# A memory-augmented recurrence beside a dense layer: ring of five places and 20 streamed units in place of six and 21, with parts of the attention later and the last eviction on two engines

## The chip, the cores and the metric

The kernel runs on one core of one Trainium2 chip. The metric is the device time of one execution in microseconds; the median of three runs before the change is 2274.5 us (2267.7 to 2279.35). A core has a matrix engine (TensorE, "PE"; "PEld" is its loading of weights), VectorE ("DVE"), ScalarE ("ACT"), GpSimd ("POOL") and SyncE ("SP"), which here only issues transfers. Matrix products accumulate in PSUM[...]; all other tiles lie in SBUF.

## The reference

The output is the sum of the input x, a recurrent attention over segments of 32 rows, and a dense layer with a gelu. The recurrent part decides the shape of the kernel. x has 2048 rows of 1024, so there are 64 segments; each has 8 rows of memory ahead of its 32 rows, and the memory rows of its output are the memory of the next segment.

```python
xn = _layernorm(x)
mem = mem0                                   # (1, 8, 1024)
for s in range(64):
    h = concatenate([mem, xn[:, 32*s:32*s+32]], axis=1)       # 40 rows
    q, k, v = (einsum('btd,dhe->bhte', h, W) for W in (Wq, Wk, Wv))   # 32 heads of 128
    scores = where(mask, einsum('bhqe,bhke->bhqk', q, k) * 128 ** -0.5, -1e9)
    o = einsum('bhqk,bhke->bhqe', softmax(scores), v)
    o = einsum('bhte,hed->btd', o, Wo)
    mem = o[:, :8]                           # the next segment waits for this
    outs.append(o[:, 8:])
return x + concatenate(outs, axis=1) + (gelu(xn @ w1 + b1) @ w2 + b2)
```

Wq, Wk, Wv and Wo are 8 MB each in bf16. They are needed whole in each of the 64 segments, and not all of the 32 MB fits into SBUF beside the rest.

## The kernel before

The dense layer comes first, up to about 443 us. Then the recurrence runs, segment after segment. A segment passes through 64 weight units of 512 KB in a fixed order: the first halves of K, Q and V (8 units each), the second halves of K, Q and V, then 16 units of the output product. Most units are resident in SBUF. The others, marked S in a string of 64 places, are streamed from DRAM each time through a ring of places. The ring and the residents share the same space: 41 places of one size and 8 late ones, 49 in all, so each place taken from the ring holds one more resident unit.

```python
STREAMED = 21
STREAM_BUFS = 6
PLACED = "S..S...S" "...S..S." "..S..S.." "S...S..S" "..S..S.S" "..S..S.." "S..S..S." ".S..S..S"
# the fourth streamed unit of a pass is kept in PSUM and put into its place from there
IN_PSUM = [unit for unit in ORDER if IS_STREAMED[unit]][3]

    def start_stream():
        if started < len(streams):
            t = slab(STREAM_PLACES[started % STREAM_BUFS])
            if streams[started] == IN_PSUM and "kept" in nxt:
                nc.scalar.copy(out=t[:, 0:1024], in_=nxt["kept"][:, 0, :])            # line 190
                nc.vector.tensor_copy(out=t[:, 1024:2048], in_=nxt["kept"][:, 1, :])  # line 191
            else:
                nc.sync.dma_start(out=t[:, :], in_=copies[streams[started]])          # line 193
            stream_tiles.append(t)
            started += 1

    def unit_done(unit):
        if IS_STREAMED[unit]:
            start_stream()       # the place just used takes the next unit that isn't under way
            ...
```

A half pass multiplies 24 rows of the segment and the 8 memory rows with eight units. The rows that a segment leaves over (8 of its 32) are gathered for four segments and go through one of the passes again with their own accumulator: with K when the segment's number is 0 modulo 4, in the output product at 1, with Q at 2 and with V at 3. The small work of the attention is put between units by number:

```python
    for i in range(KT):                       # 8 units
        t = unit_tile((w, i, u))
        product(i, t, hT, ps, range(KT))      # 4 matmuls, line 598
        if left and i not in ahead:
            product(i, t, hL, psL, order)
        unit_done((w, i, u))
        for fn in at.get(i, ()):              # small work after unit i
            fn()
```

The small work: `turn_*` turns evicted rows by four transposes into PSUM (line 555) and VectorE copies them out (lines 642 to 652); `scores` builds the scores and ScalarE takes the exponential (line 696); `sums` adds them up by a product, then a logarithm and an exponential on ScalarE (708, 709) and two products on VectorE (710, 711); `values` multiplies by V (722, 728) and both engines evict (734, 735); `keep_q` copies queries of the left rows aside (667).

```python
            at = {1: [sums]}                                # in the second half of K
            if left_q and not first:
                at[3] = [lambda: keep_q(0)]
                at[5] = [lambda: turn_qL(st["natL"], 0)]
            psK1, psK1L = half_pass("K", 1, left_k, at)
            ...
            at = {1: [sums], 4: [lambda: values(1, 0)], 6: [lambda: values(1, 1)]}   # in the output product
            ...
            for n, unit in enumerate(O_UNITS):              # 16 units
                t = unit_tile(unit)
                o_product(unit, t, psX)                     # 8 or 4 matmuls, line 746
                unit_done(unit)
                for fn in at.get(n, ()):
                    fn()
                if n == 7 and not st.get("res"):
                    load_res("e", nc.scalar)
            nw = 2 if left_o else 1                         # left_o: with left rows, one segment in four
            if not final:
                o_sb = HOME["d"]
                nc.scalar.copy(out=o_sb[:, 0:256], in_=psX[:, 0:256])                  # line 840
                if left_o:
                    nc.vector.tensor_copy(out=o_sb[:, 256:512], in_=psX[:, 256:512])   # line 842
                put_mem(o_sb, nxt["hT"], tr, 4 // nw)       # transposes (222), VectorE's copy (223)
```

`put_mem` writes the new memory rows into the rows of the next segment (`hr`), so the next segment's first product waits for it.

Of the kernel before, what the change touches and what calls it, by code (L numbers as in the profile page):

```python
# [17 lines left out]
S = 2048  # L18
# [23 lines left out]


NUNIT = 64
STREAMED = 21
STREAM_BUFS = 6


def pass_order():

    order = []

    for u in range(2):
        for w in ("K", "Q", "V"):
            for i in range(KT):
                order.append((w, i, u))
    for ch in range(2):
        for j in range(4):
            for u in range(2):
                order.append(("O", ch * 4 + j, u))  # L60
    return order


ORDER = pass_order()
PLACED = "S..S...S" "...S..S." "..S..S.." "S...S..S" "..S..S.S" "..S..S.." "S..S..S." ".S..S..S"
IS_STREAMED = {unit: PLACED[n] == "S" for n, unit in enumerate(ORDER)}
assert PLACED.count("S") == STREAMED
RESIDENT = [unit for unit in ORDER if not IS_STREAMED[unit]]

IN_PSUM = [unit for unit in ORDER if IS_STREAMED[unit]][3]  # L70
assert len(RESIDENT) == NUNIT - STREAMED


@with_exitstack
def kernel(
# [16 lines left out]
    nc = tc.nc  # L92
# [28 lines left out]
    def slab(place):  # L121
        return slabs.tile([P, 2048], BF16, name="u", tag=place)
# [14 lines left out]
    for m, n, base in ((mask_order[0:NX, 0:NX], NX, 0), (mask_order[0:SEG, NX:SEG], NL, NX)):  # L137
        nc.gpsimd.affine_select(
            out=m, in_=m, pattern=[[1, n]], compare_op=ALU.is_ge, fill=MASKED, base=base, channel_multiplier=-1,
# [3 lines left out]
        out=m, in_=m, pattern=[[-8, GRP]], compare_op=ALU.is_ge, fill=MASKED, base=0, channel_multiplier=1,  # L143
    )
    nc.gpsimd.affine_select(
        out=m, in_=m, pattern=[[8, GRP]], compare_op=ALU.is_ge, fill=MASKED, base=7, channel_multiplier=-1,
# [10 lines left out]
    PLACES += [f"w2_{k}" for k in range(14)] + [f"gT{k}" for k in range(7)]  # L157
    STREAM_PLACES, RES_PLACES = PLACES[:STREAM_BUFS], PLACES[STREAM_BUFS:]
    res_tiles = {}
# [25 lines left out]
    def start_stream():  # L185
        nonlocal started
# [3 lines that stand above are left out]
                nc.scalar.copy(out=t[:, 0:1024], in_=nxt["kept"][:, 0, :])  # L190
                nc.vector.tensor_copy(out=t[:, 1024:2048], in_=nxt["kept"][:, 1, :])
            else:
                nc.sync.dma_start(out=t[:, :], in_=copies[streams[started]])
            stream_tiles.append(t)
            started += 1
# [34 lines left out]
    with tc.tile_pool(name="ma", bufs=2) as ma, tc.tile_pool(name="mps", bufs=6, space=PSUM) as mps:  # L230
# [11 lines left out]
        o_sb = HOME["d"]  # L242
# [131 lines left out]
        for tg in range(4):  # L374
# [13 lines left out]
            for fb in range(FC):  # L388
                ps = mps.tile([P, 512], F32, name="ps")
                for kt in range(KT):  # L390
# [9 lines left out]
                    out=xb[:, :], in_=ps[:, :], func=ACT.Identity, bias=b1col[:, fb:fb + 1], scale=1.0  # L400
# [4 lines left out]
                    out=u[:, :], in0=u[:, :], scalar1=0.044715, scalar2=1.0, op0=ALU.mult, op1=ALU.add  # L405
# [47 lines left out]
            else:  # L453


                for _ in range(STREAM_BUFS):
                    start_stream()
# [35 lines left out]
    with tc.tile_pool(name="late", bufs=1) as late, \  # L493
# [16 lines left out]
        def let_go(ps):  # L510
            free_banks.append(bank_of.pop(id(ps))[0])
# [40 lines left out]
        def turn4(nat, dst):  # L552

            for c in range(4):
                nc.tensor.transpose(dst[:, c, :], nat[:, c * P:(c + 1) * P], ident[:, :])  # L555

        def by_head(t):
            return t.rearrange("p c (j t) -> p (c j) t", j=4)
# [8 lines left out]
        for s in range(NSEG):  # L567
# [14 lines left out]
            left_o = i4 == 1 or final  # L582
# [3 lines left out]
            st = {}  # L586
# [34 lines left out]
            def home(tag, pool=sp):  # L621
                return HOME[tag][:, 0:512] if tag in HOME else pool.tile([P, 512], BF16, name="natL", tag=tag)[:, :]
# [7 lines left out]
            def left_out(psL, tag, pool=sp):  # L630
                nat = home(tag, pool)
                nc.vector.tensor_copy(out=nat[:, :], in_=psL[:, :])  # L632
                let_go(psL)
                return nat

            def left_values(u, ps):
                VL[u] = left_out(ps, f"VL{u}", late)
# [6 lines left out]
            def turn_kL(nat, u):  # L644
                turn4(nat, tr)
                kL[u] = sp.tile([P, 16, 32], BF16, name=f"kL{u}")
                nc.vector.tensor_copy(out=kL[u][:, :, :], in_=by_head(tr))
# [6 lines left out]
            def turn_qL(nat, u):  # L654
                turn4(nat, qL[:, 4 * u:4 * u + 4, :])
# [9 lines left out]
            def keep_q(u):  # L665

                nc.vector.tensor_copy(
                    out=qS[:, u, :, :], in_=by_head(qL[:, 4 * u:4 * u + 4, :])[:, :, 3 * NL:4 * NL]
                )
# [44 lines left out]
            def values(u, r):  # L714

                V, prA, prB = st["V"], st["prA"], st["prB"]
                av = [new_acc() for _ in range(2)]
                oV = [t[:, 0:160].rearrange("p (c q) -> p c q", q=40) for t in av]
                for c in range(4):
                    for b in range(2):  # L720
                        q = slice(64 * r + 32 * b, 64 * r + 32 * b + 32)
                        nc.tensor.matmul(  # L722
                            oV[b][:, c, :], lhsT=V[q, c * P:(c + 1) * P], rhs=prA[q, c, :],
                            start=(c == 0), stop=False, skip_group_check=True, tile_position=(64 * r + 32 * b, 0),
                        )
                    for b in range(2):
                        q = slice(64 * r + 32 * b, 64 * r + 32 * b + 32)
                        nc.tensor.matmul(  # L728
                            oV[b][:, c, NX:40], lhsT=VL[u][q, c * P:(c + 1) * P], rhs=prB[q, c, :],
                            start=False, stop=True, skip_group_check=True, tile_position=(64 * r + 32 * b, 0),  # L730
                        )
                for b, cp in enumerate((nc.scalar.copy, nc.vector.tensor_copy)):
                    hs, t0 = slice(8 * r + 4 * b, 8 * r + 4 * b + 4), SEG + NL * slot
                    cp(out=(o_both if left_o else o_main)[u][:, hs, 0:32], in_=oV[b][:, :, 0:32])  # L734
                    cp(out=o_both[u][:, hs, t0:t0 + NL], in_=oV[b][:, :, 32:40])
                    let_go(av[b])
# [21 lines left out]
            at = {3: [lambda: turn_k(nat)]}  # L758
# [5 lines left out]
            at = {2: [lambda: turn_q(natq)], 6: [lambda: scores(0)]}  # L764
# [9 lines left out]
                left_values(0, psVL)  # L774


            at = {1: [sums]}
            if left_q and not first:
                qS = sp.tile([P, 2, 16, NL], BF16, name="qS")
                at[3] = [lambda: keep_q(0)]  # L780
                at[5] = [lambda: turn_qL(st["natL"], 0)]
            psK1, psK1L = half_pass("K", 1, left_k, at)
            natk1 = rows_out(psK1, "d")
            at = {2: [lambda: turn_k(natk1)], 4: [lambda: values(0, 0)], 6: [lambda: values(0, 1)]}
            if left_k:
                at[2].append(lambda: st.update(natL=left_out(psK1L, "d")))
                at[4].insert(0, lambda: turn_kL(st["natL"], 1))
            if left_v and not first:
                at[6].append(lambda: left_values(0, psVL))
            psQ1, psQ1L = half_pass("Q", 1, left_q, at)  # L790
            natq1 = rows_out(psQ1, "b")
            at = {3: [lambda: turn_q(natq1)], 6: [lambda: scores(1)]}
# [20 lines left out]
            psV1, psV1L = half_pass("V", 1, left_v, at)  # L813
# [4 lines left out]
                load_x_rows(s + 1, nc.gpsimd)  # L818


            at = {1: [sums], 4: [lambda: values(1, 0)], 6: [lambda: values(1, 1)]}
            if left_v and not first:
                at[6].append(lambda: left_values(1, psV1L))
            if left_q and not first:
                at[7] = [lambda: keep_q(1)]
                at[8] = [lambda: st.update(natL=left_out(psQ1L, "d"))]
                at[11] = [lambda: turn_qL(st["natL"], 1)]
            psX = new_acc()
            for n, unit in enumerate(O_UNITS):
                t = unit_tile(unit)  # L830
                o_product(unit, t, psX)
                unit_done(unit)
                for fn in at.get(n, ()):
                    fn()
                if n == 7 and not st.get("res"):
                    load_res("e", nc.scalar)
            nw = 2 if left_o else 1
            if not final:
                o_sb = HOME["d"]
                nc.scalar.copy(out=o_sb[:, 0:256], in_=psX[:, 0:256])  # L840
                if left_o:
                    nc.vector.tensor_copy(out=o_sb[:, 256:512], in_=psX[:, 256:512])
                put_mem(o_sb, nxt["hT"], tr, 4 // nw)
            res, rows = st["res"], slice(s * SEG, s * SEG + NX)
            tiles = (res, st["resL"]) if left_o else (res,)
# [12 lines left out]
            if final:  # L858
                engines = [nc.sync, nc.scalar, nc.gpsimd]
                n = 0  # L860
# [62 lines left out]
```

The softmax here doesn't subtract the row's maximum and nothing guards it: scores larger than these inputs give would overflow.

## Time and profile before

| what | before |
|---|---|
| time, median of 3 runs | 2274.5 us |
| span of the profiled execution | 2273.2 us |
| TensorE busy, share of the span | 2028.4 us, 89% |
| weight loads busy | 1047.3 us, 46% |
| VectorE busy | 828.8 us, 36% |
| ScalarE busy | 660.5 us, 29% |
| GpSimd busy | 269.6 us, 12% |
| moved by DMA | 761.91 MB |
| products of the half passes (line 598, rows of the segment) | 12288 matmuls, 939.8 us |

The page is of one execution. A busy share is an average over the dense part and the recurrence, which have different limits, so the prediction reads the recurrence by itself. Matmuls overlap: four of 32 columns each run side by side, and the busy time of TensorE is that of their union, with modelled ends. In a line of a view, "L598" is line 598 of the kernel, "acc<-u,hr" says that the tile acc is written from u and hr, and "<-" after a wait names what ended it. Numbers of columns in a shape are elements per partition. "issue" is time in which an engine waited for nothing that the profile shows. "SPq" is SyncE's queue, which issues the stream.

### The profile page before, as it was taken

To read this page: it belongs to the slowest core of one execution; us is meant where nothing else is said; L and a number is where in the kernel's file an instruction comes from. 1 tells how busy PE (TensorE), PEld (TensorE's weight loads), DVE (VectorE), ACT (ScalarE), POOL (GpSimd) and SP (SyncE) were. 2 spreads that over 40 slices of the span, in tenths; PEclk is the share of its full clock that TensorE was granted. 3 is DMA by queue.
4 is the path that set the end of the run, shared out by engine and by line. 5 is a ranking of instruction groups with operands and counts; after the bars stand their busy time and mean duration, and the time that the engine had idled before them with its cause. 6 is when DMAs were issued, how large, how long until landed. Compare 5 with 4: busy or idle time off the path is not lost.

```text
span 2273.2 us, 79002 instructions
## 1 busy us (share of the span) xinstructions
PE 2028.4 (89%) x34707; PEld 1047.3 (46%) x34707; DVE 828.8 (36%) x2264; ACT 660.5 (29%) x1540; POOL 269.6 (12%) x527
## 2 busy tenths in 40 slices
PE   7999999888898988898989898989898889888986
PEld 3444444344444444444544444444444444444443
DVE  6574844133333333333333333333323333333332
ACT  5251623122222222222222222222222222222222
POOL 0000000024111011111111111010111111111110
PEclk9999999999999999999999999999999999999999
DMA  9621116899999999999999999999999999999997
GB/s 323 205 71 33 51 51 230 296 395 391 388 402 371 384 373 388 362 382 386 386 379 401 377 397 374 395 372 374 376 372 372 376 383 400 378 379 378 401 382 276
DMA packets 256629, 761.91 MB, mean 335 GB/s; under 512 B 50923, under 2 KB 68283, under 8 KB 256284
## 3 DMA queue, kind: packets, MB, share of 16 engines
q1 hardware_dynamic: 234748, 736.71, 85.3%
q0 software_dynamic: 16000, 16.87, 2.2%
q8 instruction: 271, 4.44, 0.8%
q10 hardware_dynamic: 5536, 3.30, 0.5%
q14 instruction: 74, 0.61, 0.1%
HBM read 742.52 MB, written 33.10 MB: 341 GB/s over the span
## 4 chain that ended last, share of the span: by engine, by line
PE 66%; DMA 24%; DVE 3%; issue 3%; ACT 3%; POOL 0%; ACTq 0%; POOLq 0%; DVEq 0%; SPq 0%
PE acc L598 30%; PE acc L746 9%; PE ps L391 9%; DMA u<-Wc_O 7%; DMA u<-Wc_K 7%; PE ps L438 6%; DMA u<-Wc_V 5%; DMA u<-Wc_Q 4%; PE mixed L555 4%; PE acc L722 2%; PE ps L471 2%; PE mixed L685 1%; DVE d_oL L632 1%; PE mixed L681 1%; ACT d_oL L840 1%
## 5 line engine op out<-in xcount | busy, mean ns | idle before, releaser
L598 PE MATMUL acc<-u,hr 128*32 128x512 bf16 x12288 | 939.8, 391 | 74.6 <-DMA u<-Wc_Q 23.6
L598 PEld LDWEIGHTS <-hr 128*32 128x32 bf16 x12288 | 315.6, 97 | 379.0 <-issue 136.8
L598 PE MATMUL acc<-u,hrL 128*32 128x512 bf16 x3072 | 304.0, 384 | 3.5 <-issue 2.4
L626 ACT CAST d_oL<-acc 128x512 bf16<-128x512 f32 x192 | 112.4, 585 | 479.5 <-PE acc L598 435.4
L391 PE MATMUL ps<-u 128*128 128x512 bf16 x896 | 196.0, 382 | 2.6 <-ACT u L297 2.6
L642 DVE COPY kT<-mixed 128x512 bf16<-128x512 bf16 x128 | 54.4, 425 | 370.0 <-PE mixed L555 370.0
L746 PEld LDWEIGHTS <-b_oL 128*32 128x32 bf16 (+1 forms) x3552 | 136.1, 115 | 74.5 <-issue 64.0
L746 PE MATMUL acc<-W_O,b_oL 128*32 128x256 bf16 (+1 forms) x2220 | 130.0, 298 | 24.9 <-issue 24.9
L438 PE MATMUL ps<-u 128*128 128x512 bf16 x672 | 147.0, 379 | 0.0
L696 ACT ACTIVATE pr<-mixed 128x224 bf16<-128x224 f32 x128 | 45.7, 357 | 332.6 <-PE mixed L691 316.5
L391 PEld LDWEIGHTS <-u 128*128 128x128 bf16 x896 | 88.1, 98 | 109.2 <-issue 4.9
L746 PE MATMUL acc<-u,d_oL 128*32 128x256 bf16 (+1 forms) x2220 | 130.8, 294 | 4.9 <-DMA u<-Wc_O 2.5
L746 PEld LDWEIGHTS <-d_oL 128*32 128x32 bf16 (+1 forms) x3552 | 118.2, 112 | 33.1 <-issue 10.6
L652 DVE COPY b_oL<-mixed 128x512 bf16<-128x512 bf16 x128 | 54.4, 425 | 207.2 <-PE mixed L555 207.2
L746 PE MATMUL acc<-u,b_oL 128*32 128x256 bf16 (+1 forms) x1332 | 94.0, 300 | 26.1 <-DMA u<-Wc_O 15.2
L555 PEld LDWEIGHTS <-d_oL 128*128 128x128 bf16 x1020 | 59.4, 98 | 124.5 <-ACT d_oL L626 54.8
L598 PEld LDWEIGHTS <-hrL 128*32 128x32 bf16 x3072 | 86.0, 97 | 66.0 <-issue 9.0
L201 POOL DMA_DIRECT2D hr<-hr_d x63 | 34.6, 548 | 611.6 <-PE acc L598 351.3
L555 PE MATMUL mixed<-ident,d_oL 128*128 128x128 bf16 x896 | 89.3, 222 | 13.1 <-DVE d_oL L632 8.6
L438 PEld LDWEIGHTS <-u 128*128 128x128 bf16 x672 | 65.3, 98 | 77.4 <-DVE g_u L407 0.4
L734 ACT CAST d_oL<-acc 128x128 bf16<-128x128 f32 x128 | 50.9, 397 | 171.7 <-PE acc L728 171.7
L399 ACT ACTIVATE g_xb<-ps,b1col 128x512 bf16<-128x512 f32 x112 | 76.9, 686 | 61.0 <-PE ps L391 59.9
(126 smaller groups left out, 2408.4 us busy)
## 6 DMA issues: line engine op xcount, KB each, us to landing
u<-Wc_K SPq DMA_DIRECT2D x384, 512.0 KB
u<-Wc_O SPq DMA_DIRECT2D x384, 512.0 KB
u<-Wc_Q SPq DMA_DIRECT2D x257, 512.0 KB
u<-Wc_V SPq DMA_DIRECT2D x256, 512.0 KB
u<-in_B_w_dram SPq DMA_DIRECT2D x16, 448.0 KB
u<-in_B_w_dram SPq DMA_DIRECT2D x14, 512.0 KB
u<-in_A_Wv_dram SPq DMA_DIRECT2D x12, 512.0 KB
u<-in_A_Wq_dram SPq DMA_DIRECT2D x11, 512.0 KB
```

The costliest lines, as they stand in the source:

```text
L391: nc.tensor.matmul(ps[:, :].rearrange("p (s t) -> p s t", t=SEG), lhsT=w1_sb[fb // 14 * 8 + kt][:, (fb % 14) * P:(fb % 14 + 1) * P], rhs=x ...
L399: nc.scalar.activation(out=xb[:, :], in_=ps[:, :], func=ACT.Identity, bias=b1col[:, fb:fb + 1], scale=1.0)
L438: nc.tensor.matmul(ps[:, :], lhsT=gts[fc // 4][:, fc % 4, t * P:(t + 1) * P], rhs=w2_sb[fc // 2][:, fc % 2, cs], start=(fc == 0), stop=(fc ...
L471: nc.tensor.matmul(pss[2 * t + nb][:, :], lhsT=gts[fc // 4][:, fc % 4, t * P:(t + 1) * P], rhs=w2_sb[fc // 2][:, fc % 2, nb * 512:nb * 512 ...
L555: nc.tensor.transpose(dst[:, c, :], nat[:, c * P:(c + 1) * P], ident[:, :])
L598: nc.tensor.matmul(acc[32 * j:32 * j + 32, :], lhsT=lhs[:, i, :], rhs=t[:, 512 * j:512 * j + 512], start=(i == seq[0]), stop=(i == seq[-1] ...
L626: nc.scalar.copy(out=nat[:, :], in_=ps[:, :])
L642: nc.vector.tensor_copy(out=st["kT"][:, :, :], in_=by_head(tr))
L652: nc.vector.tensor_copy(out=st["qT"][:, :, 0:32], in_=by_head(tr))
L696: nc.scalar.activation(out=pr[:, :], in_=mixed[:, 0:224], func=ACT.Exp, scale=INV_SQRT_DH)
L734: cp(out=(o_both if left_o else o_main)[u][:, hs, 0:32], in_=oV[b][:, :, 0:32])
L746: nc.tensor.matmul(acc[r:r + n // 8, 0:n], lhsT=lhs[:, 4 * (i % 4) + 2 * u + k, :], rhs=t[:, 1024 * k + n * jq:1024 * k + n * jq + n], sta ...
```

## The change

It takes one place from the ring (five in place of six) and makes the unit that fits there resident, so a pass streams 20 units in place of 21; one of them is still refilled from PSUM. The streamed units are placed anew in the order. The sums and the kept and turned queries in the second half of K come later by one or two units. In the output product the values come after units 5 and 7 in place of 4 and 6, keeping the queries moves from unit 7 to 8, and so does loading the rest of the output (`res`). In the segments that take left rows through K, the first values in the second half of Q come one unit later. The last eviction of a segment, by ScalarE alone in three segments of four, is split into halves for ScalarE and VectorE. It is for less traffic, fewer waits for small work and a shorter end of a segment.

```diff
-STREAMED = 21
-STREAM_BUFS = 6
+STREAMED = 20
+STREAM_BUFS = 5
@@
-PLACED = "S..S...S" "...S..S." "..S..S.." "S...S..S" "..S..S.S" "..S..S.." "S..S..S." ".S..S..S"
+PLACED = "S...S..." "S...S..S" "...S..S." "..S...S." ".S..S..S" "..S..S.." "S..S..S." ".S..S..S"
@@
-            at = {1: [sums]}
+            at = {2: [sums]}
             if left_q and not first:
                 qS = sp.tile([P, 2, 16, NL], BF16, name="qS")
-                at[3] = [lambda: keep_q(0)]
-                at[5] = [lambda: turn_qL(st["natL"], 0)]
+                at[5] = [lambda: keep_q(0)]
+                at[7] = [lambda: turn_qL(st["natL"], 0)]
             psK1, psK1L = half_pass("K", 1, left_k, at)
@@
             at = {2: [lambda: turn_k(natk1)], 4: [lambda: values(0, 0)], 6: [lambda: values(0, 1)]}
             if left_k:
                 at[2].append(lambda: st.update(natL=left_out(psK1L, "d")))
-                at[4].insert(0, lambda: turn_kL(st["natL"], 1))
+                at[5] = at[4]
+                at[4] = [lambda: turn_kL(st["natL"], 1)]
@@
-            at = {1: [sums], 4: [lambda: values(1, 0)], 6: [lambda: values(1, 1)]}
+            at = {1: [sums], 5: [lambda: values(1, 0)], 7: [lambda: values(1, 1)]}
             if left_v and not first:
-                at[6].append(lambda: left_values(1, psV1L))
+                at[7].append(lambda: left_values(1, psV1L))
             if left_q and not first:
-                at[7] = [lambda: keep_q(1)]
-                at[8] = [lambda: st.update(natL=left_out(psQ1L, "d"))]
+                at[8] = [lambda: keep_q(1), lambda: st.update(natL=left_out(psQ1L, "d"))]
                 at[11] = [lambda: turn_qL(st["natL"], 1)]
@@
-                if n == 7 and not st.get("res"):
+                if n == 8 and not st.get("res"):
@@
             if not final:
                 o_sb = HOME["d"]
-                nc.scalar.copy(out=o_sb[:, 0:256], in_=psX[:, 0:256])
-                if left_o:
-                    nc.vector.tensor_copy(out=o_sb[:, 256:512], in_=psX[:, 256:512])
+                n = 256 * nw
+                nc.scalar.copy(out=o_sb[:, 0:n // 2], in_=psX[:, 0:n // 2])
+                nc.vector.tensor_copy(out=o_sb[:, n // 2:n], in_=psX[:, n // 2:n])
                 put_mem(o_sb, nxt["hT"], tr, 4 // nw)
```

## The prediction

> **What bounds the kernel now.** I read four views: the page, the busy time in the recurrence alone, TensorE's waits there, and a piece of the chain of waits.
>
> The page first: the share of the DMA engines in 40 slices, and the chain that ended last.
>
> ```profile
> DMA  9621116899999999999999999999999999999997
> PE 66%; DMA 24%; DVE 3%; issue 3%; ACT 3%; POOL 0%; ACTq 0%; POOLq 0%; DVEq 0%; SPq 0%
> ```
>
> The DMA engines are full from the ninth slice on, which is the recurrence over 64 segments; before it they have slack. The chain passes through TensorE and transfers and hardly through anything else. The busy time of the recurrence by itself (engines with their busy us, then granted clock, DMA share, GB/s):
>
> ```profile
> core 0: us, PE busy (x) PEld busy (x) DVE busy (x) ACT busy (x) POOL busy (x), PEclk, DMA share, GB/s
> 471.00:2230.00 1759.00, 1561.63 (x31648) 828.09 (x31647) 566.77 (x1609) 483.55 (x1240) 253.49 (x476) 0.98 1.00 383
> ```
>
> The first and last eviction of a segment's end (line 840, the first at 471.4, the last at 2230.2) are 62 segments apart, so a segment takes 1758.8/62 = 28.37 us. In it the DMA engines have a share of 1.00: no slack. TensorE's waits between 500 and 2230 us, that is in 1730/28.37 = 61 segments (who, for whom: us in total, times, longest):
>
> ```profile
> PE acc L746 <- issue: 38.9, 30, 2.5
> PE mixed L222 <- ACT d_oL L840: 28.7, 61, 0.5
> PE acc L598 <- DMA u<-Wc_Q: 20.4, 38, 1.6
> PE acc L598 <- DMA u<-Wc_K: 18.2, 45, 1.4
> PE acc L746 <- DMA u<-Wc_O: 17.4, 36, 1.0
> ...
> PE acc L722 <- DVE pr L710: 10.8, 33, 0.6
> PE mixed L555 <- DVE d_oL L632: 8.6, 15, 0.6
> PE acc L598 <- DMA u<-Wc_V: 7.8, 18, 1.5
> PE qL L555 <- DVE qS L667: 5.3, 14, 0.4
> ```
>
> The four DMA lines sum to 63.8 us, 1.05 us a segment. Without them TensorE would need 28.37 - 1.05 = 27.3 us. So two limits lie one microsecond apart: transfers at 28.4, TensorE at 27.3. Last, one turn of a place of the ring, in the chain (start, us, what):
>
> ```profile
> 1833.91 7.87 DMA u<-Wc_K
> 1841.78 0.04 issue
> 1841.82 1.26 PE acc L598 x20
> ...
> 1847.62 7.82 DMA u<-Wc_V
> ```
>
> From issue to landing a 512 KB unit takes 7.9 us here; the chain's transfers of stream units between 1000 and 2240 us lie between 5.7 and 9.0, mostly near 7.5. A place comes round after 6 of the 20 transfers of a segment, 28.37 x 6/20 = 8.5 us; 7.5 of it is the transfer and its queue, 1.0 the unit's use and its wait for it.
>
> **What the Trainium skill says.** "DMA: Bandwidth & Descriptors", section "Issuing engines are not separate DMA queues", says that transfers of all issuing engines run on the same 16 engines and interleave. The trace agrees: one share of 1.00 covers the stream and all small transfers. The same page, "Where 436 GB/s comes from", puts the ceiling of the port side at 435 GB/s and the memory side of one core at about 358. The 383 GB/s here are above the second figure, so the measurement decides: I take 383 as what this mix reaches when full. "Perfetto Trace Analysis", "What 'DMA-bound' means", separates full DMA engines from a full issuing sequencer; SPq has 0% of the chain, so here it is the engines. "Runtime: NRT & Kernel Launch", "Instruction fetch mechanics", says that an engine's instructions arrive by DMA in blocks of 16 KiB. The page's instruction queue q8 (271 packets, 4.44 MB, so 16.4 KB each) agrees in size. The 38.9 us of "issue" may be such fetches; that is a guess, and nothing in the change removes them.
>
> **The change part by part.**
>
> *One unit less by DMA.* Of 21 streamed units one is refilled from PSUM, so 20 come by DMA, 19 after. A segment now moves 383 x 28.37 = 10.87 MB, of which 20 x 0.524 = 10.49 MB is the stream. After: 10.34 MB, at 383 GB/s 27.0 us. The transfer limit falls by 1.37 us, to below TensorE's 27.3.
>
> *Ring of five.* With the engines full, one transfer fewer lies ahead of each new one: landing 7.5 - 1.37 = 6.1 us, plus 1.0 of use is 7.1. A turn of five of 19 at 27.0 us gives 27.0 x 5/19 = 7.1. So the ring just holds; what it had as a reserve is gone. Jitter that six places hid now shows as waits. I choose 0.5 us of DMA waits a segment after, half of today's 1.05.
>
> *Sums, values, turns later.* They leave the work as it is. At most they take away the waits on VectorE's products (10.8), the kept queries (5.3), and 1.4 for the exponential (line 704): 17.5 us/61 = 0.29 us a segment. I credit 0.25, since the sums of half one stay at unit 1 of the output product and one kind of segment brings its values closer together.
>
> *The end's eviction by two engines.* Today ScalarE copies 256 columns in 0.372 us. Split, it copies 128 in 0.265 and VectorE 128 in 0.292 (rows of line 734, same shape). Side by side that would save 0.08. But where it is split already (after every fourth segment) VectorE waits for ScalarE each time:
>
> ```profile
> L842 DVE CAST d_oL<-acc x16: 424/424/425, 500.5 to 2203.7; 128x256 bf16<-128x256 f32 x16
> its engine sat idle before it (us, times) until:
>   ACT d_oL L840: 20.1, 16
> ```
>
> and in the order of instructions of the changed kernel every such copy waits for ScalarE's. One after the other is 0.265 + 0.03 + 0.292 = 0.59, which is 0.21 longer.
>
> *A shift that the diff does not name.* The refill from PSUM is set off by the release of a place. The unit is the fourth streamed one of a pass, so before it is started by streamed unit 21 + 4 - 6 = 19 of 21, unit 9 of the 16 of the output product (from 0), after by 20 + 4 - 5 = 19 of 20, unit 12. It occupies ScalarE, then VectorE:
>
> ```profile
> L190 ACT COPY u<-kept x63: 1012/1012/1013, 469.6 to 2228.8; 128x1024 bf16<-128x1024 bf16 x63
> L191 DVE COPY u<-kept x63: 691/692/693, 470.6 to 2229.8; 128x1024 bf16<-128x1024 bf16 x63
> ```
>
> ScalarE is held until 1.06 us after unit 12, VectorE until 1.78. The three units left take 3 x 0.22 = 0.66 us (0.43 each in a segment with left rows). The end's eviction thus queues behind the refill: its VectorE half would end at 1.78 + 0.29 = 2.07 us in place of 0.70 + 0.37 = 1.07. That is up to 1.0 us on TensorE's path in three segments of four, less where the last units were late by a transfer or an "issue" wait anyway. I choose 0.4 as the mean over all segments, the 0.21 of above within it.
>
> *Sum.* TensorE: 27.3 - 0.25 + 0.4 = 27.45; DMA waits 0.5; together 27.95 us, 0.42 less than now. Times 64 segments is 27 us; the dense part before 443 us is untouched. 2274.5 - 27 = 2247; the load on the engines being lower I allow a few us for shorter landings: 2244.
>
> **The rivals.**
>
> *TensorE alone decides, and the ring is deep enough.* Transfers at 27.0 leave nothing to wait for, the queues are shorter, and the refill hides. Then a segment takes about 27.1 to 27.2 us, and the whole 2195 to 2200. For it: a full unit of traffic goes, with a DMA share of 1.00 before. Against it: landings of 6.1 us in a turn of 7.1.
>
> *The ring binds.* If the landing does not shorten by the missing unit (7.5 us stays), a turn is 8.5 us and a segment 8.5 x 19/5 = 32 us; even half of that, 7.9 a turn, is 30 us, 2380. Against it: the engines are full, so most of those 7.5 us must be queue, and the small GpSimd loads (64 KB) land in 5.2 to 5.6 us in the same crowd. A mild form, 7.3 us a turn, gives 27.7 us, about where I am.
>
> *The end of the segment binds.* The full 1.0 us in three segments of four adds 0.75 a segment: TensorE 27.8, with the waits 28.3, time as before (2270). For it: VectorE's refill waited for ScalarE's in 58 of 63 cases. Against it: the transfers catch up during such a stall, so it replaces DMA waits rather than adding to them.
>
> **Range and chances.** 2244 is what the terms give. The first rival mixed in sets the low end, 2208; the third, or a slightly too shallow ring, the high end, 2274. Faster by over 2% needs under 2229, 0.24 us a segment better than my sum: 0.28. Slower by over 2% needs the ring to bind outright: 0.06. Between them 0.66.
>
> **What would show it.** In the changed kernel's profile: the period between end evictions near 27.95 us; the DMA share over the recurrence at 0.97 to 0.99, not 1.00; DMA waits of TensorE near 30 us in total against 63.8 (at 60 or more the ring is too shallow); the chain's pieces of transfer near 6 us; waits of line 222 for the end's eviction at 45 us or more against 31.5 (28.7 for ScalarE's copy and 2.8 for VectorE's), now on VectorE's copy; the waits for line 710 and line 667 nearly gone. The prediction is wrong if the landing stays above 6.7 us, if the refill at the end costs nothing, or if the DMA share stays at 1.00 with more time a unit.

## The result, and the profile after

The changed kernel takes 2337.2 us (median of 6 runs) against 2272.1 us for the kernel before in the same comparison: ratio 1.0274, 95% interval 1.0233 to 1.0315. It is slower by 65 us, where the prediction had it a little faster, at 2244.

The page of the changed kernel: the DMA engines in 40 slices, the chain by engine, the chain by line.

```profile
DMA  9521117899999999999999999999999999999997
PE 57%; DMA 33%; ACT 4%; DVE 4%; issue 2%; POOL 0%; ACTq 0%; POOLq 0%; SPq 0%; DVEq 0%
PE acc L598 26%; DMA u<-Wc_Q 13%; DMA u<-Wc_O 10%; PE ps L391 8%; PE ps L438 6%; DMA u<-Wc_K 6%; PE acc L746 6%; DMA u<-Wc_V 4%; PE mixed L555 3%; PE acc L722 2%; PE ps L471 2%; ACT u L190 1%; ACT d_oL L735 1%; ACT d_oL L734 1%; DVE u L191 1%
```

Transfers now take a third of the chain (24% before), although there is less to transfer. The slices look as before; the digits are too coarse to tell. The busy times of the recurrence (columns as in the prediction):

```profile
471.00:2290.00 1819.00, 1603.64 (x31700) 844.28 (x31701) 580.31 (x1658) 480.04 (x1244) 253.40 (x476) 0.97 0.96 353
```

353 GB/s at a share of 0.96, against 383 at 1.00. The engines are no longer full, and the kernel waits for transfers more than before. The end's evictions (line 841) start at 474.9 first and 2293.0 last, so a segment takes 1818.1/62 = 29.32 us, 0.95 more than before. TensorE's waits in the 1790/29.32 = 61 segments between 500 and 2290 us:

```profile
PE acc L746 <- DMA u<-Wc_O: 50.1, 85, 2.2
PE acc L598 <- DMA u<-Wc_Q: 33.0, 60, 1.5
PE mixed L222 <- ACT d_oL L841: 24.0, 61, 0.5
PE acc L598 <- DMA u<-Wc_K: 23.7, 32, 1.6
PE acc L746 <- issue: 13.3, 16, 2.2
...
PE acc L598 <- DMA u<-Wc_V: 9.7, 16, 1.4
PE mixed L222 <- DVE d_oL L842: 6.4, 31, 0.4
...
PE qL L555 <- DVE qS L667: 1.6, 7, 0.5
```

The DMA lines sum to 116.5 us, 1.91 us a segment against 1.05. This rise of 0.86 us is nearly as large as the 0.95 us that a segment has become longer, but it is not the whole account. The "issue" waits fell by 25.6 us, 0.42 a segment, and the busy time of TensorE rose, from 1561.63/62 = 25.19 us a segment to 1603.64/62.04 = 25.85. The section on why the prediction was wrong comes back to both. A piece of the chain (start, us, what) shows what such a wait looks like, and the end of a segment:

```profile
1302.17 7.71 DMA u<-Wc_Q
...
1323.86 1.02 ACT u L190
1324.90 0.69 DVE u L191
1325.60 0.40 DVE d_oL L842
...
1327.92 8.28 DMA u<-Wc_V
```

These two transfers take 7.7 and 8.3 us, with one transfer fewer that could lie ahead of them. They are among the long ones: the chain passes through 77 stream transfers between 1000 and 2290 us, with a median of 6.8 us (49 with 7.55 us between 1000 and 2240 us before). Between the two stands the queue at the end that the prediction described: the refill on ScalarE, the refill on VectorE, then VectorE's half of the eviction. Over the whole trace this queue is small. ScalarE's half starts within 0.05 us of the last product in all 63 segments. VectorE's half always follows it, as the prediction said, and comes later than that by more than 0.02 us in 22 segments, by 0.28 us at most and 3.1 us in all.

### The profile page after: what moved, and what is told of

Read it like the earlier page. It is cut to its first block, busy times and chain, and to the rows that moved or that the text cites. A ratio compares the mean times of both kernels' runs of the same rounds, so it can differ in the third digit from the quotient of the medians.

```text
span 2335.2 us, 78748 instructions
## 1 busy us (share of the span) xinstructions
PE 2072.1 (89%) x34687; PEld 1063.2 (46%) x34707; DVE 841.4 (36%) x2311; ACT 656.1 (28%) x1540; POOL 269.5 (12%) x527
## 4 chain that ended last, share of the span: by engine, by line
PE 57%; DMA 33%; ACT 4%; DVE 4%; issue 2%; POOL 0%; ACTq 0%; POOLq 0%; SPq 0%; DVEq 0%
PE acc L598 26%; DMA u<-Wc_Q 13%; DMA u<-Wc_O 10%; PE ps L391 8%; PE ps L438 6%; DMA u<-Wc_K 6%; PE acc L746 6%; DMA u<-Wc_V 4%; PE mixed L555 3%; PE acc L722 2%; PE ps L471 2%; ACT u L190 1%; ACT d_oL L735 1%; ACT d_oL L734 1%; DVE u L191 1%
## 5 line engine op out<-in xcount | busy, mean ns | idle before, releaser
L598 PE MATMUL acc<-u,hr 128*32 128x512 bf16 x12288 | 968.5, 400 | 91.3 <-DMA u<-Wc_Q 36.4
L598 PEld LDWEIGHTS <-hr 128*32 128x32 bf16 x12288 | 327.5, 99 | 422.2 <-issue 179.0
L746 PEld LDWEIGHTS <-b_oL 128*32 128x32 bf16 (+1 forms) x3552 | 129.7, 113 | 83.8 <-issue 72.8
L746 PEld LDWEIGHTS <-d_oL 128*32 128x32 bf16 (+1 forms) x3552 | 125.8, 112 | 36.9 <-issue 19.0
L191 DVE COPY u<-kept 128x1024 bf16<-128x1024 bf16 x63 | 43.6, 692 | 150.7 <-ACT u L190 145.3
```

The lines of the kernel that those rows point to most:

```text
L598: nc.tensor.matmul(acc[32 * j:32 * j + 32, :], lhsT=lhs[:, i, :], rhs=t[:, 512 * j:512 * j + 512], start=(i == seq[0]), stop=(i == seq[-1] ...
L746: nc.tensor.matmul(acc[r:r + n // 8, 0:n], lhsT=lhs[:, 4 * (i % 4) + 2 * u + k, :], rhs=t[:, 1024 * k + n * jq:1024 * k + n * jq + n], sta ...
```

## The experiments

Three theories stand against each other. Theory R says that the ring decides: a place fewer costs more than a unit less gives. Theory E says that the end of a segment decides, by the split eviction and the refill that starts late. Theory M says that the small work collides at its later places. Each edit is given against the changed kernel unless said otherwise. Four runs take the change apart first.

**The ring alone.** The kernel before with the three lines of the ring changed.

```diff
-STREAMED = 21
-STREAM_BUFS = 6
+STREAMED = 20
+STREAM_BUFS = 5        # and the new PLACED; all else as before
```

> The kernel before with only the ring changed: five places, 20 units, the new placement; small work and the end's eviction as before. Theory R (one place fewer costs more than one unit less gives): the whole loss is here, 2325 to 2350 us. Theory E (the end of the segment: the split eviction and the refill from PSUM that now starts three units before the end): the split is undone but the refill still starts late, so part of the loss goes, about 2300 to 2315. Theory M (the small work placed later collides): 2245 to 2275, as the moves are not in it.

Measured 2326.4 us, ratio to before 1.0249 (1.0200 to 1.0297). Nearly the whole loss is in these lines, as R said.

**The moves alone.**

```diff
-STREAMED = 20
-STREAM_BUFS = 5
+STREAMED = 21
+STREAM_BUFS = 6        # and the old PLACED; small work and eviction as in the changed kernel
```

> The changed kernel with the ring of before: six places, 21 units, the old placement; the small work later and the split eviction stay. Theory R: within 10 us of before, 2260 to 2280, a little faster if the waits for line 710 are gone. Theory E: the split eviction costs 0.2 us in three of four segments, about 10 us, hidden behind full transfer engines, so 2270 to 2285. Theory M: 2310 or more.

The time is 2282.7 us, ratio 1.0052 (1.0029 to 1.0074). This is a small loss, just above the range of R and within that of E. M is out as the main cause.

**Six places, 20 units.** This kernel leaves out one unit's own weights: that unit shares another's place, and the space goes to the ring.

```diff
-STREAM_BUFS = 5
+STREAM_BUFS = 6
-            return res_tiles[unit]
+            return res_tiles[RESIDENT[len(RES_PLACES) - 1] if unit == shared else unit]
         late_units = deque(RESIDENT[len(RES_PLACES):])
+        shared = late_units.pop()
```

> The changed kernel with a sixth place and still 20 units streamed. Room is made by letting the last resident unit of the output product share the place of another resident unit, so that unit's own weights are left out and its product uses others; the work and its order are the same. The refill from PSUM then starts after unit 9 of the output product, as in the kernel before. Theory R: DMA waits of TensorE fall under 0.5 us a segment, a segment takes 27.3 to 27.6 us, 2200 to 2225 us. Theory E: faster as well, as the refill is early again, but only to 2270 to 2290. Theory M: stays at 2325 or more.

The time is 2244.8 us, ratio 0.9880 (0.9851 to 0.9910). One place more turns the loss into a gain, though less of one than R named (2200 to 2225).

**Five places, 21 units.**

```diff
-STREAMED = 20
+STREAMED = 21          # and the old PLACED; a place of SBUF stays empty
```

> The changed kernel with five places but 21 streamed units in the old placement, so the traffic of before through the shallower ring (one place of SBUF stays empty). The refill starts after unit 12 of the output product. Theory R: a place comes round in 7.3 us in the changed kernel; at the same turn 20 transfers need 20 x 7.3 / 5 = 29.2 us plus the refill's share, so a segment takes 30.4 to 31 us, 2400 to 2445 us. Theory E or M: the traffic adds little, 2340 to 2365.

The time is 2395.2 us, ratio 1.0543 (1.0509 to 1.0576). It is just under R's range of 2400 to 2445 and far above that of E and M. With the same small work these runs make a square: a place fewer costs 1.0543 - 1.0052 = 4.9% at 21 units and 1.0274 - 0.9880 = 3.9% at 20; a unit less gives 2.7% with five places and 1.7% with six. The change buys the second with the first. The cost of a place is measured at the same streamed units. A unit less comes with the new placement of the streamed units, and no run has the new placement at 21 units or the old one at 20, so the gain of a unit includes what the placement does. (With six places the refill starts after unit 9, with five after unit 12; the next run takes that apart.)

**The late refill.** The third streamed unit of a pass is the one kept in PSUM, so its refill starts after unit 9 of the output product as in the kernel before.

```diff
-IN_PSUM = [unit for unit in ORDER if IS_STREAMED[unit]][3]
+IN_PSUM = [unit for unit in ORDER if IS_STREAMED[unit]][2]
```

> The changed kernel, but the third streamed unit of a pass is the one kept in PSUM, in place of the fourth. The refill then starts after unit 9 of the output product, as in the kernel before, and no longer stands in the way of the end's eviction. Ring, traffic and moves as in the changed kernel. Theory E (the late refill costs): the waits for the end's eviction fall back, about 0.2 us a segment, 2320 to 2328. Theory R (the ring decides, 20 fills of five places, so a segment is four turns of 7.3 us): TensorE only waits for a transfer in place of the eviction, 2332 to 2342.

The time is 2325.7 us, ratio 1.0254 (1.0210 to 1.0298), beside 1.0274 (1.0233 to 1.0315) for the changed kernel. It lies in the range of E and under that of R, but the intervals overlap. What the late refill costs as a whole isn't separated from nothing here; it is at most a small part of the loss.

**The refill by DMA.** As much traffic as before, through five places.

```diff
-            if streams[started] == IN_PSUM and "kept" in nxt:
+            if False:
```

> The changed kernel without the refill from PSUM: the unit comes by DMA like the others, so a segment moves 20 units by DMA through five places, as much traffic as before. If the ring counts fills (a refilled place is held for a turn like any other), the segment stays four turns of 7.2 to 7.4 us, 28.8 to 29.6 us, 2300 to 2350 us: a unit more by DMA costs nothing. If the traffic counts, the step from 20 to 21 units measured with this ring (2337 to 2395) comes again: 2385 to 2405.

The time is 2339.9 us, ratio 1.0314 (1.0271 to 1.0358). This is the run that decides. Twenty transfers a segment in place of 19 add 0.0040 to the ratio, and the intervals overlap, where going from 20 units to 21 with this ring added 0.0269. The edit also takes the refill off ScalarE and VectorE, but starting the refill early gave only 0.0020, so this can't hide a cost of 0.0269. (The profiled execution is the slowest of four, 2353 us; its 29.62 us a segment are 0.3 above the changed kernel's for that reason in part.) The busy times between 1000 and 2200 us:

```profile
1000.00:2200.00 1200.00, 1051.69 (x20612) 549.75 (x20616) 349.96 (x1035) 268.50 (x762) 143.55 (x272) 0.95 0.98 364
```

The engines carry 364 GB/s here, against 351 in the same stretch of the changed kernel, so those 351 were not all they could carry. What is short is not the engines but the number of fills that five places can make, and a refill from PSUM is a fill too.

**Small work later, one engine evicts.** The kernel with the moves alone, with the end's eviction as before.

```diff
-                nc.scalar.copy(out=o_sb[:, 0:n // 2], in_=psX[:, 0:n // 2])
-                nc.vector.tensor_copy(out=o_sb[:, n // 2:n], in_=psX[:, n // 2:n])
+                nc.scalar.copy(out=o_sb[:, 0:256], in_=psX[:, 0:256])
+                if left_o:
+                    nc.vector.tensor_copy(out=o_sb[:, 256:512], in_=psX[:, 256:512])
```

> Ring and placement of before and the small work at its new places, with the end's eviction by ScalarE alone as before. The same with the split took 2283 against 2272 before. If the split costs (0.2 us in three segments of four): 2268 to 2275, no slower than before. If the later places of sums and values cost: 2278 to 2288.

The time is 2278.9 us, ratio 1.0038 (1.0016 to 1.0060). So the later places cost some 0.4% with the ring of before. The split adds 0.0014 to the ratio, which the intervals don't separate from nothing.

**The refill out of turn.** The kernel of the first run; the PSUM unit is started three places later, by VectorE alone, into whichever place has just come free.

```diff
+    per_pass = [unit for unit in ORDER if IS_STREAMED[unit]]
+    rest = [unit for unit in per_pass if unit != IN_PSUM]
+    at_psum = per_pass.index(IN_PSUM) + 3
+    streams = per_pass + (rest[:at_psum] + [IN_PSUM] + rest[at_psum:]) * (NSEG - 1)
@@ a freed place is taken by the next start, not the next in a circle
-                nc.scalar.copy(out=t[:, 0:1024], in_=nxt["kept"][:, 0, :])
+                nc.vector.tensor_copy(out=t[:, 0:1024], in_=nxt["kept"][:, 0, :])
```

> Ring of five places with 20 units, small work and the end's eviction as before (2326 with the refill in its turn). The start of the PSUM unit is put off by three places: it is started two streamed units ahead of its use in place of five, by VectorE alone (2 x 0.69 us), and the transfers behind it start one place earlier each. The same work and traffic. If fills are what counts, the refill holds a place for 2 of 5 parts of a turn, a segment is (19 + 0.4) / 5 = 3.88 turns of 7.3 us = 28.3 us in place of 29.2, about 2255 to 2285. If only the number of transfers and their landing count, it stays at 2315 to 2335.

The time is 2304.4 us, ratio 1.0145 (1.0104 to 1.0187) against 1.0249 (1.0200 to 1.0297) with the refill in its turn. The other order of the starts gives back 1% with the same transfers. It is in the direction that counting fills asks for, but some 20 us short of the range (28.78 us a segment; 3.88 turns of 7.3 would be 28.3). The edit also takes the refill out of the segment's end and off ScalarE, which this run doesn't separate. Why it falls short was not taken apart; a likely reason, not shown, is that where another wait than the ring ends a stretch, a place that is free sooner gains nothing.

**Four places, and seven.** One timed run each, so without an interval; with seven places two units' own weights are left out.

```diff
-STREAM_BUFS = 5
+STREAM_BUFS = 4        # IN_PSUM is the third streamed unit, so the refill starts after unit 12
```

> The changed kernel with four places and 20 streamed units (one place of SBUF stays empty); the third streamed unit is the one refilled from PSUM, so the refill still starts after unit 12. Landing was 6.6 us in the mean with six places and 6.1 with five. If a landing is mostly a fixed part (the quickest twentieth takes 4.6 us with any ring), it falls little again, to 5.4 to 5.7 us; a turn is then 6.4 us with use and waits, a segment 20/4 = 5 turns = 31 to 33 us, 2440 to 2560 us. If a landing is mostly queue, as the prediction had it (1.4 us less for each place), it falls to 4.6 us, a turn to 5.7, a segment to 28.5 us, 2280 us.

The time is 2547.4 us, beside a median of 2276.7 of the kernel before. It lies in the range of a landing that hardly falls, near its upper end. The busy times between 500 and 2200 us:

```profile
500.00:2200.00 1700.00, 1399.86 (x26627) 720.26 (x26625) 484.35 (x1390) 399.58 (x1039) 210.08 (x393) 0.94 0.91 316
```

```diff
-STREAM_BUFS = 5
+STREAM_BUFS = 7        # two units share others' places; IN_PSUM is the fifth streamed unit
```

> The changed kernel with seven places and 20 streamed units; two resident units use the weights of two others, whose places they share, so two units' own weights are left out. The fifth streamed unit is refilled from PSUM, so the refill starts after unit 9. If six places (27.9 us a segment) still left the ring short: 27.2 to 27.5 us, 2200 to 2220 us. If TensorE is the bound with six already: 27.7 to 27.9 us, 2232 to 2248 us.

The time is 2224.9 us, between the two ranges. TensorE's waits for transfers between 500 and 2200 us are nearly gone:

```profile
PE acc L599 <- DMA u<-Wc_Q: 1.4, 5, 0.4
PE acc L599 <- DMA u<-Wc_K: 1.4, 2, 1.0
PE acc L599 <- DMA u<-Wc_V: 0.9, 3, 0.4
PE acc L747 <- DMA u<-Wc_O: 0.6, 2, 0.3
```

They sum to 4.3 us. A segment takes 27.65 us. This is TensorE with its other waits, at 20 units and with the small work of the change. By this one run the ring of six, at 27.92, still cost some 0.3 us.

**Six places, 20 units, old small work.** One unit's own weights are left out, as in the run with six places above; small work and eviction are those of the kernel before.

> Six places and 20 units with the placement of the change (one unit's own weights left out, as in the run with six places before), but the small work and the end's eviction as in the kernel before. Here neither ring nor transfers are at their limit, so what the later small work is worth on TensorE shows. The prediction credited the later places with 0.25 us a segment and debited the split eviction: with both as before 2240 to 2260 us against 2245. If the later places only cost, as with the full ring (7 to 11 us): 2230 to 2240 us.

The time is 2238.0 us, ratio 0.9840 (0.9812 to 0.9868) against 0.9880 (0.9851 to 0.9910) with the changes to both. The intervals overlap, but a gain of 0.25 us a segment (16 us) from the moves is not there. Its waits, in this kernel's line numbers (711 is VectorE's product of line 710, 668 the kept queries):

```profile
PE acc L723 <- DVE pr L711: 14.1, 41, 0.3
...
PE qL L556 <- DVE qS L668: 6.0, 15, 0.4
```

With the later places, the run with six places above has

```profile
PE qL L556 <- DVE d_oL L633: 3.8, 15, 0.3
...
PE qL L556 <- DVE qS L668: 2.6, 14, 0.2
```

and no line for the product. So 17.5 us of these waits go and 3.8 us come new on line 633, but the time doesn't follow. The granted clocks show a cost of the same size. In the 52 executions of the kernel before that were run beside these experiments, the clock is 0.982 in the mean, and a clock lower by 0.01 goes with a time longer by 15 us. The two kernels with the later places and the old ring had 0.976; at that clock the 52 executions give 2280.5 us, and the two take 2282.4 and 2280.1 us in the mean. Here it is 0.977 with the later places and 0.982 without, an estimate of 8 us where 6.8 were measured. So the small loss of the later places goes with a lower clock. Why the clock is lower was not found, and no run sets it by itself.

## Why the prediction was wrong

The following table compares the runs. A fill is anything that is put into a place of the ring, by DMA or by the refill. A turn is the time after which a place takes its next fill. The landing of a transfer is taken from the trace's semaphore records (last update of a transfer less its issue, mean of all between 600 and 2200 us). The period is the time of a segment, from the end's evictions. The turn is worked out as period x places / fills.

| kernel | places | fills a segment (by DMA) | landing, us | turn, us | period, us |
|---|---|---|---|---|---|
| four places | 4 | 20 (19) | 5.56 | 6.54 | 32.70 |
| changed | 5 | 20 (19) | 6.08 | 7.33 | 29.32 |
| refill by DMA | 5 | 20 (20) | 6.19 | 7.41 | 29.62 |
| 21 units | 5 | 21 (20) | 6.16 | 7.21 | 30.28 |
| before | 6 | 21 (20) | 6.60 | 8.11 | 28.37 |
| six places | 6 | 20 (19) | 6.44 | 8.38 | 27.92 |
| seven places | 7 | 20 (19) | 6.66 | 9.68 | 27.65 |

Since the turn comes from the period, the table can't by itself confirm that a segment is fills / places turns. That rests on forecasts made from a turn before the runs: 30.4 to 31 us a segment with 21 units, 28.8 to 29.6 with the refill by DMA, 31 to 33 with four places. Measured are 30.28, 29.62 and 32.70, in the ranges or within 0.15 us of them. What the table adds is the part of a turn that isn't landing. It is 1.0 to 1.25 us with four and five places, 1.5 and 1.9 with six, and 3.0 with seven, where the ring no longer binds and places wait.

**The step that failed is "Ring of five": that the ring just holds, with 0.5 us of DMA waits a segment.** Measured are 1.91 us. The difference of 1.41 us times 64 segments is 90 us, and the prediction was 2337 - 2244 = 93 us off. Two things were wrong in the step. The count gives 1.4 of the 2.3 us between its 27.0 and the measured 29.32, the turn the other 0.9.

*The count of the turns.* The prediction divided 19 transfers by five places. The refill from PSUM takes its place for a turn as well, so 20 fills count, and a segment is 4 turns, not 3.8. Its own 7.1 us a turn would then have given 28.4 us where it read 27.0, which is no gain on the 28.37 of before. The refill by DMA shows the count: a fill's kind hardly matters.

*The landing.* The prediction took full engines to mean that most of the 7.5 us is queue, and a place fewer to take 1.37 us off it. The 7.5 us were read from the chain, which passes through the late transfers; over all transfers the mean is 6.60. A place fewer took off about half of what was counted on, or less: 0.77 us of the chain's median (7.55 to 6.78), 0.52 of the mean (6.60 to 6.08). At 20 units the mean fell by 0.36 us from six places to five and by 0.52 from five to four. A twentieth of the landings is shorter than 4.3 to 4.9 us, whatever the ring. That the prediction wrote 6.1 and the mean is 6.08 is no hit, as one was read from the chain and the other over all. The loads of 64 KB (`hr`), which it took for a sign of queue, have a median of 5.4 us before, and of 5.6 with five places and with four; they don't shorten with the ring either. With 1.25 us for use, release and waiting landed, a turn of five is 7.33 us, and 4 x 7.33 = 29.3. The rival "the ring binds" named this. Its mild form of 7.3 us a turn was right, and led to 27.7 us only because the fills were counted wrongly there too.

*What would show it* was named in part rightly: DMA waits of 60 us or more in total mean that the ring is too shallow, and they are 116.5. The share, 0.96, is just under the 0.97 named. The landing, which was to stay under 6.7 us, lies on both sides of it by the two measures, 6.08 and 6.78.

**The transfer limit** of 27.0 us isn't contradicted: no run comes below it. It is not what decides at five places.

**TensorE's side** came out near the sum of its terms, 29.32 - 1.91 = 27.41 us against 27.45, but not by those terms, so this agreement is luck.

- The waits for lines 710 and 667 nearly went, as said, some 0.24 us a segment.
- Line 222 has 30.4 us in all, not 45. The split is one half after the other, as foretold, but the refill delays VectorE's half by 3.1 us in all 63 segments together, not by a part of 1.0 us in each. TensorE waits for the late evictions no more than before.
- "Issue" fell from 38.9 to 13.3 us, 0.42 us a segment, which nothing in the prediction foresaw. Its guess of instruction fetches fits the trace: before, each of the 28 "issue" waits of over 0.6 us between 500 and 2230 us ended 1.2 to 1.5 us after the end of a 16 KB packet of the instruction queue. On the output product, from 500 to 2200 us, these waits sum to 48.2 us with seven places, 41.6 with six at 20 units, 37.3 before and 11.1 in the changed kernel; with four places there is no such line. So they go where TensorE waits for transfers. That a fetch then lies hidden behind such a wait is likely, but no run isolates it.
- TensorE's busy time rose by 0.66 us a segment, as worked out above. The granted clock fell from 0.982 to 0.968 in the mean of the executions. With the 15 us for 0.01 from above, that is an estimate of some 20 of the 65 us. No run separates it from the ring: the clock is also lower the shorter the ring (0.977, 0.968 and 0.946 with six, five and four places at 20 units), so it may be a consequence. A lower clock alone is not the cause of the loss, since the kernel with six places has 0.977 and is faster than the one before.

**The late refill and the split** are small here: 0.2% and 0.1% of ratio, neither clear of the intervals. **The later small work** saves nothing in any pair and costs 0.4% with the ring of before. It goes with a lower granted clock, whose cause stays open.

A kernel with six places and 20 units would beat both, with 2238 us and the small work of before. It leaves out one unit's own weights to get the space, so it isn't a complete kernel; whether a place can be found elsewhere was not tried. Of the complete kernels none beats the one before.

## What to carry to other kernels

While a ring binds, it is sized by fills: period = fills / places x (landing + use), and every fill counts that passes through a place, from DRAM or not. Take the landing from the trace, over all transfers and not only those of the chain, and don't count on it to shrink by a whole transfer's time when a place goes: here it shrank by 0.4 to 0.5 us where 1.37 were counted on. Full DMA engines don't show that the landing is queue. Trading a prefetch buffer for less traffic pays only while the turn still fits, so make both divisions first: here 3.5 turns of 8.1 us became 4 turns, which had to fit into 28.37/4 = 7.1 us to break even and took 7.3.

## What the runs showed of the hardware

The share of the DMA engines is the time of packets, not the pace: 353 GB/s at 0.96 is 368 scaled to a full share, and 316 at 0.91 is 347, both under the 383 at 1.00. A ring that is short of transfers loses pace while its engines still look nearly full. A landing of a 512 KB unit never came near the 1.4 us (28.37/20) at which units follow one another before: the shortest in the traces takes 3.4 us, and the mean stayed at 5.6 us even with four places.

In the clock records of these traces TensorE has its full clock or half of it and nothing between, half mostly for stretches of 3.4 us. Between 500 and 2200 us such stretches sum to 82 us in the kernel before and 123 us in the changed one.
